# New order table, two loads swapped, copies split by PSUM bank, last tile in halves: one transformer block on one core

## The chip, the cores and the metric

The kernel runs on one core of one Trainium2 chip. The metric is the device time of one execution in microseconds (us). A core has five engines that run their own instruction streams: PE (TensorE, the matrix unit; its weight loads are counted apart as PEld), DVE (VectorE), ACT (ScalarE), POOL (GpSimd) and SP (SyncE, which only issues DMAs here). They wait for one another through semaphores. Each instruction stream is executed in order, so a waiting instruction holds up all that stands behind it on its engine.

## The reference

x has 2048 rows of 448 columns (bf16). One block is an attention with a learned feature map, and then a gated MLP that mixes over the rows; both are modulated by six vectors from a conditioning row c.

```python
mod = (silu(c) @ w_mod).reshape(1, 6, 1, 448)   # sa, ca, ga, sb, cb, gb
h = layernorm(x) * (1 + ca) + sa
x = x + ga * A(h)
h = layernorm(x) * (1 + cb) + sb
x = x + gb * B(h)

def A(h):        # 16 heads of 28
    q, k, v = split(h @ wqkv)
    phi(t) = concat(softmax(t @ w_phi), softmax(-(t @ w_phi)))   # per head
    kv, z = einsum(phi(k), v), sum over rows of phi(k)
    return (phi(q) @ kv) / (phi(q) @ z + 1e-6) @ wo

def B(h):
    z = gelu(h @ w_in)                     # 1792 columns
    z1, z2 = z[:896], layernorm(z[896:])
    return (z1 * (w_sp @ z2 + b_sp)) @ w_out
```

## The kernel before

The rows are cut into 16 tiles of 128 (number i below). The work runs in four stages.

1. Setup. The first loads go out on two DMA rings: ACT's (line 608: the last 64 rows of Wk, 56 KB; 610: x tiles 0 and 1, 224 KB; 611: part of w_mod) and SP's (607 c, 609 the other 384 rows of Wk, 613 w_phi, then w_mod, x and the weights of v and q through `load_rows`, which loads a 64-row piece and a 384-row piece). PE runs warm-up matmuls (`keep_busy`) and then `fold_T`: 16 transposes of Wk into two PSUM banks (`tps[0]` for groups g = 0 and 1, `tps[1]` for g = 2 and 3) and four copies out (line 742). Meanwhile DVE takes the statistics of x tiles 0 and 1, POOL makes the reciprocal deviations (`l1_rstd`, lines 680 to 684) and a product BD of w_phi with a mask (line 788), DVE applies the normalisation (line 690), and PE transposes the tiles (`turn_mm`; `turn_out` copies them into hT). `fold_pf` multiplies Wk by w_phi; `fold_W` scales the result into Wk. `columns` makes the modulation columns; `sapad`, `fold_sa` and the copy at 816 bring the shift into the last row of Wk's factor.
2. Keys and values, 3. attention output and 4. z. These are not written as loops but as a list of words, `ORDER`, which a loop at line 1191 plays: each word calls one step for one tile. The engine streams take their instructions in the order of this list, so the list fixes the order on each of the five engines at once.
5. Gating and output: for each of four column blocks of w_sp seven groups g_ps of 16 matmuls (line 1213), and 16 output tiles o_ps (1220). Tile 15 is the last: eight matmuls of 448 columns, the left half copied by ACT (1265), the right half by DVE (1267), each with its own store.

The words of the list, by engine:

- PE: k, v (key and value matmuls of a tile), kv (adds phi(k) x v into the accumulator kvacc), tm (transposes of an x tile), fq (transposes of Wq), sq, pq, bv, cfb, gt, gr, wb, zb (small matmuls for weights and biases), qp and q (queries), num (phi(q) @ kv), wo (output projection), z2 and z1 (the two halves of h @ w_in)
- ACT: e (two exponentials of k), vc (copies v), wv.0, wv.1 and bvc (the scaled value weights), gs (squares of Wk or Wq, lines 955 and 956; they only serve a flag that checks a bound), fqc, sqc, pqc, cfc, gtc, wbc, zbc, grc, qpe, qe (exponentials of q), sx, ge and zg (gelu), zn (normalises z2)
- DVE: bn, ag (statistics of x), ld1 (normalises tile 2 or 3), to, wv.2, wv.3, rd, rc, mu (softmax of k), wg, ws (scales wo and w_in), kb1, kb2 (kvacc into KVbd), cr, dn, ri, w, t (divides num), xc (adds the residual), ls, la, zs, za (statistics)
- POOL: rp, rs (reciprocal deviations), la1, ap (normalises a tile into a padded buffer), ad (adds the two halves of t into one of three buffers opad), ca, cc (constants)
- SP: ld (loads; 3 is x tiles 12 to 15, 4 is 840 KB of w_mod, 7 and 9 are 392 KB of it, 5 and 6 w_in, 8 wo), lT, oT, h2T (transposes of a tile by DMA: into hT, from opad, from the second layernorm), wsp.0 (eight transposing loads of w_sp's first block; they must all be there before g_ps starts)

A tile of the attention output goes num, sx, cr, dn, ri, w, t, ad, oT, wo, xc; then ls, la, rs, ap, h2T, z2, ge, zs, za; zn of tile i uses the rs of i + 3 (`ZL = 3`), and h2T of tile i + 3 comes out of the same rs. PSUM has a pool of four single banks (tag B: k, v, q, z1, wo and the small ones) and one of two double banks (tag A: kvacc, qp, num, z2); PE waits when the slot that it is to write has not been read yet. num.i holds its double bank until t.i.

Of the kernel before, what the change touches and what calls it, by code (L numbers as in the profile page):

```python
# [1320 lines left out]
```

## Time and profile before

| | us |
|---|---|
| median of 4 runs | 263.78 (262.85 to 264.59) |
| the profiled execution: device time | 263.19 |
| the profiled execution: span from first to last instruction | 261.4 |
| PE busy | 250.5 |
| DVE busy | 163.7 |
| PE busy at full clock, 20 to 60 | 40.0 of 40 |
| start of g_ps | 137.1 |
| end of the last matmul, about | 255.6 |

The page gives the busy time of each engine and its share; the windows give the same for a stretch. "Idle before" is the time an engine stood still ahead of an instruction, with the one that released it. The chain of waits is followed back from the last instruction: each row is a piece of time in which the end was held by that instruction. Ends of matmuls are modelled by the profiler, so two matmul rows may overlap by a tenth or two. The granted PE clock is 0.999 of full speed over the span.

### The profile page before, as it was taken

The numbers are of one execution on the slowest core, as the hardware profiler recorded it, in microseconds if no ns is written. First come the engines' busy times: TensorE is split into PE (matmuls) and PEld (weight loads), VectorE is DVE, ScalarE is ACT, GpSimd is POOL, SyncE is SP. The second block draws the span as 40 slices with busy tenths as digits, with TensorE's granted clock in tenths as the row PEclk, the third lists the DMA queues.
The fourth block names the chain that finished last, engine by engine and source line by source line (L and its number), as shares of the span: only waits on it lengthen the run. The fifth ranks groups of instructions, "written<-read, shape, count | busy, mean of one in ns | idle before, by whom it ended". The sixth has DMA issues, their size and how long they took to land.

```text
span 261.4 us, 4432 instructions
## 1 busy us (share of the span) xinstructions
PE 250.5 (96%) x1590; PEld 129.4 (50%) x1590; DVE 163.7 (63%) x364; ACT 107.9 (41%) x208; POOL 90.3 (35%) x201
## 2 busy tenths in 40 slices
PE   6889999999998999999999999999999999999991
PEld 3655666675554555544444444444444444444440
DVE  2889989999999989978062464432542534342540
ACT  2599777979775478887985000000000000000000
POOL 4787871004888778756340083000000000000000
PEclk9999999999999999999999999999999999999999
DMA  7975899506556334144499999950000010001002
GB/s 179 292 210 96 162 182 137 197 3 63 116 118 89 63 61 63 32 90 82 85 208 187 226 168 183 184 119 29 18 0 18 20 35 0 0 24 32 19 20 63
DMA packets 69057, 25.29 MB, mean 97 GB/s; under 512 B 59105, under 2 KB 68898, under 8 KB 69026
## 3 DMA queue, kind: packets, MB, share of 16 engines
q1 hardware_dynamic: 68066, 24.12, 46.2%
q10 hardware_dynamic: 960, 0.80, 1.1%
q8 instruction: 14, 0.23, 0.4%
q14 instruction: 17, 0.14, 0.2%
HBM read 8.92 MB, written 1.84 MB: 41 GB/s over the span
## 4 chain that ended last, share of the span: by engine, by line
PE 83%; DVE 6%; DMA 3%; ACT 3%; issue 2%; POOL 1%; ACTq 0%
PE g_ps L1213 37%; PE z_ps L832 17%; PE o_ps L1220 8%; PE v_ps L832 4%; PE k_ps L832 4%; PE x_ps L1105 3%; PE kvacc L866 3%; PE q_ps L832 2%; DVE t L1074 2%; DMA f_x<-in_A_x_dram 2%; DMA oT<-f_opad 2%; PE num L1045 2%; PE b_ps L778 1%; ACT f_Wsq L955 1%; ACT f_E L839 0%
## 5 line engine op out<-in xcount | busy, mean ns | idle before, releaser
L1213 PE MATMUL g_ps<-f_wsp,f_z2n 128*128 128x512 bf16 x336 | 74.3, 379 | 0.0
L1213 PEld LDWEIGHTS <-f_z2n 128*128 128x128 bf16 x448 | 43.7, 98 | 52.0
L1215 DVE TENSOR_TENSOR gb<-g_ps,f_bsp 128x512 f32<-128x512 f32 x28 | 19.4, 691 | 67.1 <-PE g_ps L1213 67.1
L1265 ACT CAST ot<-o_ps 128x224 bf16<-128x224 f32 x1 | 0.3, 346 | 114.6 <-PE o_ps L1220 114.6
L832 PE MATMUL z_ps<-f_win,h2T 128*128 128x448 bf16 (+1 forms) x128 | 26.9, 352 | 0.5 <-DMA h2T<-f_xpad 0.3
L1128 DVE BATCH_NORM_STATS2 z2st<-z2g 128x6 f32<-128x448 bf16 x32 | 19.2, 613 | 11.5 <-ACT z2g L1167 11.4
L832 PE MATMUL z_ps<-h2T,f_win 128*128 128x512 bf16 x112 | 26.2, 379 | 0.0
L1213 PE MATMUL g_ps<-f_hT,f_z2n 128*128 128x512 bf16 x112 | 25.0, 379 | 0.0
L1080 POOL TENSOR_TENSOR f_opad<-t 128x448 bf16<-128x448 bf16 x16 | 16.8, 1057 | 23.5 <-DVE t L1074 22.9
L1220 PE MATMUL o_ps<-f_wout,f_z1T 128*128 128x448 bf16 x112 | 23.5, 352 | 0.0
L1216 DVE TENSOR_TENSOR f_z1T<-gb,f_z1T 128x512 bf16<-128x512 f32 x28 | 21.1, 752 | 1.0
L1178 ACT ACTIVATE f_z1T<-z_ps,f_b 128x512 bf16<-128x512 f32 x28 | 18.2, 683 | 3.7 <-PE z_ps L832 3.7
L850 DVE TENSOR_REDUCE ksum<-f_E 128x32 f32<-128x896 bf16 x16 | 16.8, 1073 | 1.7 <-ACT f_E L839 1.5
L1171 ACT ACTIVATE f_z2n<-z2g,nm,rs 128x896 bf16<-128x896 bf16 x16 | 17.8, 1128 | 0.3 <-POOL nm L1142 0.3
L832 PEld LDWEIGHTS <-h2T 128*128 128x128 bf16 (+1 forms) x128 | 12.0, 97 | 11.8 <-DMA h2T<-f_xpad 0.8
L1167 ACT ACTIVATE z2g<-z_ps 128x896 bf16<-128x896 f32 x16 | 14.6, 919 | 6.6 <-PE z_ps L832 5.3
L832 PEld LDWEIGHTS <-f_win 128*128 128x128 bf16 x112 | 10.9, 97 | 12.8
L1074 DVE TENSOR_TENSOR t<-num,w 128x896 bf16<-128x896 f32 x16 | 17.0, 1084 | 0.1
L839 ACT ACTIVATE f_E<-k_ps 128x448 bf16<-128x448 f32 x32 | 16.1, 561 | 1.8 <-issue 1.1
L1220 PEld LDWEIGHTS <-f_z1T 128*128 128x128 bf16 x112 | 11.0, 98 | 10.9
L832 PEld LDWEIGHTS <-f_hT 128*128 128x128 bf16 (+1 forms) x128 | 11.5, 97 | 8.7 <-issue 0.5
L832 PE MATMUL v_ps<-f_Wv,f_hT 128*128 128x448 bf16 x64 | 14.6, 352 | 0.4 <-ACT junk L968 0.4
(148 smaller groups left out, 339.6 us busy)
## 6 DMA issues: line engine op xcount, KB each, us to landing
out_dram<-ot SPq DMA_DIRECT2D x15, 112.0 KB, 1.7
f_x<-in_A_x_dram SPq DMA_DIRECT2D x3, 448.0 KB, 7.0
f_win<-in_B_w_in_dram SPq DMA_DIRECT2D x2, 672.0 KB, 5.1
f_wm<-in_w_mod_dram SPq DMA_DIRECT2D x1, 840.0 KB, 6.9
f_wout<-in_B_w_out_dram SPq DMA_DIRECT2D x1, 784.0 KB, 6.0
f_bsp<-in_B_b_sp_dram SPq DMA_DIRECT2D x1, 512.0 KB, 5.0
f_wm<-in_w_mod_dram ACTq DMA_DIRECT2D x1, 448.0 KB, 6.1
f_wm<-in_w_mod_dram SPq DMA_DIRECT2D x1, 392.0 KB, 7.0
```

Source lines behind the costliest of these rows:

```text
L832: nc.tensor.matmul(out, lhsT=lhs(kc, last[kc]), rhs=rhs(kc, last[kc]), start=(kc == 0), stop=(kc == KC - 1))
L839: nc.scalar.activation(out=Ering[i % NR][:, s, :], in_=ps["k", i][:, 0:D], func=ACT.Exp, scale=1.0 - 2.0 * s)
L850: nc.vector.tensor_reduce(out=cs["s", i][:], in_=Ering[i % NR][:].rearrange("p s (c f h) -> p (s c) h f", c=4, h=HP), axis=AX.X, op=ALU.add)
L1074: nc.vector.tensor_tensor(out=ts[i][:, 0:2 * D].rearrange("p (s h d) -> p s h d", s=2, h=H), in0=nv(i)[:, :, :, 0:DH], in1=cs.pop(("w", i) ...
L1080: nc.gpsimd.tensor_tensor(out=opad[i % NO][:, 0:D], in0=t[:, 0:D], in1=t[:, D:2 * D], op=ALU.add)
L1128: nc.vector.bn_stats(out=cs["z", i][:, hf, :], in_=z2gs[i][:, hf * D:(hf + 1) * D])
L1171: nc.scalar.activation(out=z2n[:, i, :], in_=z2gs.pop(i)[:], func=ACT.Identity, scale=rstd[:, 1:2], bias=nmr[:, 1:2])
L1178: nc.scalar.activation(out=z1T[:, fc, st * 512:(st + 1) * 512], in_=ps.pop(("z1", st, fc)), func=ACT.Gelu_apprx_tanh, bias=b1[:, fc:fc + 1])
L1213: nc.tensor.matmul(g[:], lhsT=z2n[:, s_, fc * P:(fc + 1) * P], rhs=wsp_tiles[tcn][:, s_, :], start=(s_ == 0), stop=(s_ == NT - 1))
L1215: nc.vector.tensor_tensor(out=gb[:], in0=g[:], in1=bsp[:, tsl], op=ALU.add)
L1216: nc.vector.tensor_tensor(out=z1T[:, fc, tsl], in0=gb[:], in1=z1T[:, fc, tsl], op=ALU.mult)
L1220: nc.tensor.matmul(o_ps, lhsT=z1T[:, fc, t * P:(t + 1) * P], rhs=wout_s[:, fc, :], start=(first and fc == 0), stop=(fc == FC - 1))
```

## The change

On ACT's ring, x tiles 0 and 1 are loaded ahead of the 64-row piece of Wk. `load_rows` loads its big piece ahead of the small one. In `fold_T`, ACT copies both groups of the first bank and DVE both of the second, instead of one of each. POOL makes tile 0's and 1's reciprocal deviations before BD. The transposes of tile 1 stand ahead of `fold_pf` instead of behind `columns`, its copy out goes from DVE to ACT and stands behind `fold_sa`, and a filler matmul takes the old place. The statistics of tile 3 (bn.3, ag.3) leave the list and are taken with tile 2's. The last output tile is computed as two groups of 224 columns in two banks, and each half is copied and stored behind its own group. All other words of the list are the same and stand in another order. Of the list, the rows that matter most are shown.

```diff
@@ the table ORDER @@
-cc gs.0 k.0 bv bn.3 wv.2 ag.3 wv.1 bn.4 rp.1 gr.0 bn.5 bvc k.1 ld.7 wv.0 ag.4 wv.3 ag.5 ld.3 bn.7 grc.0 sq rp.2 e.0.0 bn.6 v.0 e.1.0 ld1.3 sqc ag.7
-e.1.1 ld1.2 tm.3 ag.6 bn.10 e.0.1 fq.0 la1.5 vc.0 to.3 fq.1 ag.10 rd.0 la1.4 fqc.2 lT.5 tm.2 k.3 fqc.0 rp.3 fqc.1 to.2 gt.0 rc.0 lT.4 fqc.3 bn.8 e.3.0
-k.2 mu.0 e.3.1 la1.7 rd.1 v.3 e.2.0 la1.6 lT.7 gtc.0 v.2 bn.9 e.2.1 ag.8 rc.1 k.4 vc.3 ag.9 lT.6 mu.1 rp.4 vc.2 pq.2 rd.2 v.1 e.4.1 ld.4 pqc.2 kv.0
-bn.12 vc.1 v.4 la1.8 bn.11 e.4.0 rc.2 pq.1 lT.8 pq.3 ag.12 vc.4 ag.11 k.5 rd.3 rp.5 pqc.1 k.6 pqc.3 mu.2 e.5.0 v.5 rc.3 rd.4 e.5.1 la1.9 pq.0 kv.1
-la1.11 bn.13 v.7 vc.5 mu.3 la1.10 lT.11 pqc.0 kv.2 ag.13 bn.15 k.7 rp.6 e.6.0 rd.5 e.6.1 lT.10 kv.3 v.6 rd.6 vc.7 la1.12 lT.9 qp.0 vc.6 rc.5 la1.13
...
-vc.14 zb mu.15 vc.15 wg.2 gs.1 wg.0 kv.14 wg.1 wg.3 kv.15 wb.3 kb1 wb.2 wbc.3 kb2 gr.1 wbc.2 ws.1 num.0 zbc num.1 ws.3 sx.0 q.5 sx.1 cr.0 cr.1 dn.0
-q.4 dn.1 ri.0 ri.1 qe.5.1 w.0 w.1 t.0 grc.1 q.6 qe.5.0 t.1 qe.4.1 q.12 ad.0 qe.6.0 num.3 qe.6.1 ws.2 ad.1 oT.0 num.2 qe.4.0 ws.0 q.9 sx.3 sx.2 qe.12.1
-cr.3 wsp.0.2 cr.2 q.7 dn.3 dn.2 qe.9.1 ri.3 ri.2 w.3 w.2 qe.9.0 q.8 t.3 qe.7.0 wsp.0.5 wo.0 qe.7.1 t.2 ad.3 qe.8.0 num.4 oT.1 xc.0 ad.2 num.5 sx.4
-q.10 cr.4 ls.0 sx.5 qe.12.0 oT.2 dn.4 cr.5 q.14 la.0 dn.5 ri.4 qe.10.1 rs.0 ri.5 w.4 w.5 qe.8.1 t.4 q.11 oT.3 wo.1 t.5 ad.4 qe.11.1 num.6 qe.11.0 xc.1
-ap.0 num.7 oT.4 sx.6 qe.10.0 q.13 cr.6 ls.1 ad.5 sx.7 qe.14.0 dn.6 q.15 cr.7 h2T.0 la.1 qe.14.1 dn.7 ri.6 rs.1 ri.7 w.6 qe.13.1 w.7 wo.2 t.6 qe.13.0
-wsp.0.3 wo.3 qe.15.0 ap.1 t.7 qe.15.1 num.8 ad.6 h2T.1 xc.2 z2.0 sx.8 tb cr.8 ad.7 dn.8 xc.3 oT.6 ri.8 ls.2 wo.4 ge.0 w.8 oT.5 la.2 t.8 gt.1 rs.2
-num.9 ls.3 oT.7 z2.1 zs.0.0 ap.2 sx.9 cr.9 la.3 dn.9 ad.8 zs.0.1 h2T.2 wo.5 ri.9 za.0 ge.1 w.9 xc.4 rs.3 wo.6 oT.8 t.9 num.10 zs.1.0 z2.2 ap.3 sx.10
-zn.0 cr.10 ls.4 ad.9 h2T.3 dn.10 zs.1.1 gtc.1 wo.7 ri.10 ge.2 la.4 w.10 oT.9 za.1 t.10 wo.8 rs.4 num.11 xc.5 z2.3 zs.2.0 sx.11 ap.4 zn.1 xc.6 ad.10
-xc.8 h2T.4 z1.0.2 ge.3 zs.2.1 ls.5 z1.0.1 oT.10 za.2 la.5 cr.11 xc.7 z1.0.3 rs.5 zs.3.0 z1.0.6 dn.11 ls.6 zg.0.3 ri.11 ap.5 z2.4 zs.3.1 zg.0.6 w.11
...
-ge.11 wsp.0.0 la.13 z1.2.5 rs.13 zs.11.0 z2.12 zg.2.5 zs.11.1 xc.14 ap.13 wo.15 ls.14 ge.12 h2T.13 za.11 la.14 z1.2.1 rs.14 xc.15 zn.9 zs.12.0 z1.2.0
-ls.15 zg.1.3 z1.2.6 ap.14 zs.12.1 zg.2.1 la.15 za.12 z1.2.2 h2T.14 rs.15 zg.2.6 zn.10 z1.2.4 z2.13 ap.15 zn.11 h2T.15 zn.12 z1.2.3 wsp.0.1 zg.2.0
-z2.14 zg.2.2 zg.2.3 wsp.0.4 zg.2.4 z1.3.4 ge.13 z1.3.5 wsp.0.7 ge.14 z1.3.6 zs.14.0 z2.15 zg.3.6 zs.14.1 zg.3.4 za.14 zs.13.0 rs.17 z1.3.1 ge.15
-zs.13.1 z1.3.3 za.13 zg.3.1 rs.16 zs.15.0 z1.3.2 zs.15.1 zg.3.3 zn.14 z1.3.0 za.15 rs.18 zg.3.2 zn.13 zn.15 zg.3.5 zg.3.0
+ca wv.3 rp.1 k.1 bv wv.0 wv.2 wv.1 bn.4 k.0 bvc bn.5 e.1.1 cc ag.4 ld.4 ld1.2 e.1.0 sq ag.5 bn.7 e.0.0 v.0 ld1.3 sqc ld.7 e.0.1 ag.7 bn.6 tm.2 tm.3
+vc.0 v.1 rp.2 to.2 gs.0 rd.0 k.2 to.3 v.2 rc.0 la1.5 bn.8 vc.1 v.3 bn.10 la1.4 vc.2 ag.6 e.2.0 fq.1 mu.0 rp.3 lT.4 e.2.1 fq.0 bn.9 vc.3 kv.0 ag.8 rd.1
+fqc.0 k.3 lT.5 fqc.2 la1.6 cfb bn.11 e.3.1 la1.7 rd.2 lT.6 e.3.0 gt.0 cfc fqc.3 rd.3 k.4 gtc.0 ld.3 gr.0 fqc.1 lT.7 ag.9 rc.2 e.4.1 rp.4 v.4 rc.1 rc.3
+grc.0 mu.1 k.5 vc.4 ag.10 mu.2 e.4.0 pq.1 la1.8 v.5 ag.11 e.5.0 rd.4 e.5.1 la1.9 pq.3 lT.8 kv.1 pqc.1 pq.2 rp.5 mu.3 kv.2 pqc.3 bn.13 k.6 wsp.0.4
+pqc.2 bn.12 vc.5 kv.3 ag.13 rd.5 la1.10 pq.0 e.6.0 v.6 lT.9 pqc.0 la1.11 rc.4 k.7 ag.12 rc.5 vc.6 rp.6 lT.11 mu.4 k.8 e.7.0 bn.15 e.6.1 v.7 lT.10
...
+rc.15 kv.13 mu.15 v.15 wg.1 wg.2 kv.14 wg.0 vc.15 wb.3 qpe.1.0 kv.15 wb.2 qpe.1.1 kb2 kb1 zb wbc.3 wg.3 gr.1 ws.2 num.0 num.1 ws.1 sx.0 q.7 zbc sx.1
+cr.0 wbc.2 cr.1 dn.0 q.5 dn.1 ri.0 ri.1 qe.7.1 w.0 w.1 t.0 qe.7.0 q.4 grc.1 t.1 qe.5.1 ad.0 num.3 qe.4.0 q.6 sx.3 ws.0 qe.4.1 ad.1 oT.0 num.2 cr.3
+ws.3 q.13 sx.2 qe.6.0 oT.1 cr.2 dn.3 q.12 dn.2 qe.5.0 ri.3 ri.2 w.3 qe.6.1 w.2 t.3 q.8 qe.12.1 t.2 wo.0 ad.3 qe.8.1 num.4 qe.12.0 xc.0 ad.2 num.5 sx.4
+q.10 cr.4 sx.5 ls.0 qe.8.0 oT.2 gt.1 dn.4 cr.5 ri.4 qe.10.0 dn.5 w.4 ri.5 q.9 la.0 qe.10.1 w.5 t.4 oT.3 rs.0 qe.13.1 wo.1 qe.9.0 t.5 num.6 gtc.1 ad.4
+xc.1 sx.6 num.7 ap.0 cr.6 q.14 ls.1 sx.7 qe.9.1 ad.5 dn.6 h2T.0 cr.7 la.1 q.15 dn.7 qe.13.0 ri.6 ri.7 w.6 qe.14.1 w.7 rs.1 t.6 wo.2 oT.4 qe.15.0
+qe.14.0 t.7 num.8 ap.1 qe.15.1 oT.5 wo.3 sx.8 xc.2 ad.6 tb z2.0 cr.8 xc.3 h2T.1 ad.7 dn.8 ls.2 ri.8 wo.4 oT.6 la.2 w.8 ge.0 ls.3 rs.2 wo.5 t.8 oT.7
+num.9 ap.2 zs.0.0 z2.1 sx.9 la.3 ad.8 h2T.2 cr.9 zs.0.1 dn.9 za.0 ri.9 wo.6 rs.3 w.9 oT.8 ge.1 xc.4 wo.7 t.9 num.10 ap.3 xc.5 z2.2 sx.10 zs.1.0 ad.9
+h2T.3 cr.10 ls.4 dn.10 wo.8 zs.1.1 oT.9 ge.2 ri.10 za.1 w.10 la.4 t.10 zn.0 rs.4 num.11 z1.0.0 ls.5 sx.11 zs.2.0 z2.3 ap.4 zg.0.0 cr.11 xc.6 ad.10
+h2T.4 dn.11 zs.2.1 z1.0.2 ri.11 ge.3 la.5 za.2 w.11 xc.8 rs.5 z1.0.3 zg.0.2 t.11 zn.1 num.12 z1.0.5 zs.3.0 ap.5 ls.6 sx.12 zg.0.3 z2.4 ad.11 zs.3.1
...
+ls.15 rs.13 wo.14 ge.11 z1.2.5 xc.14 zn.8 zs.11.0 ap.13 z2.12 ls.14 zg.2.5 h2T.13 zs.11.1 la.14 z1.2.2 za.11 ge.12 rs.14 z1.2.3 zg.2.2 zs.12.0 zn.10
+z1.2.4 la.15 zs.12.1 ap.14 z1.2.0 za.12 zg.1.3 h2T.14 rs.15 zg.2.3 z2.13 zg.2.0 zg.2.4 ap.15 z1.2.1 ge.13 h2T.15 z1.2.6 zg.2.1 zs.13.0 wsp.0.1 zn.11
+z2.14 wsp.0.5 z1.3.6 ge.14 z1.3.3 wsp.0.2 zg.3.6 zs.14.0 zn.12 z2.15 zs.14.1 wsp.0.0 za.14 zs.13.1 zg.3.3 rs.17 z1.3.1 za.13 ge.15 z1.3.5 rs.16 zg.3.1
+zs.15.0 z1.3.0 zs.15.1 zg.3.5 z1.3.4 za.15 zg.3.0 rs.18 zn.14 z1.3.2 zn.13 zn.15 zg.2.6 zg.3.2 zg.3.4
```

```diff
@@ -599,15 +599,15 @@
     wmod_v = w_mod.rearrange("(k p) n -> p k n", p=DC)
 
     def load_rows(eng, dst, src):
+        eng.dma_start(out=dst[:, 0:3, :], in_=src[0:3 * P, :].rearrange("(k p) n -> p k n", p=P))
         eng.dma_start(out=dst[0:64, 3, :], in_=src[3 * P:D, :])
-        eng.dma_start(out=dst[:, 0:3, :], in_=src[0:3 * P, :].rearrange("(k p) n -> p k n", p=P))
 
 
     nc.vector.memset(wk_raw[64:P, 3, :], 0.0)
     nc.sync.dma_start(out=c_row[:], in_=c)
-    nc.scalar.dma_start(out=wk_raw[0:64, 3, 0:D], in_=A_wqkv[3 * P:D, D:2 * D])
     nc.sync.dma_start(out=wk_raw[:, 0:3, 0:D], in_=A_wqkv[0:3 * P, D:2 * D].rearrange("(k p) n -> p k n", p=P))
     nc.scalar.dma_start(out=x_sb[:, 0:2, :], in_=xv[:, 0:2, :])
+    nc.scalar.dma_start(out=wk_raw[0:64, 3, 0:D], in_=A_wqkv[3 * P:D, D:2 * D])
     nc.scalar.dma_start(out=wm1[:, :, D:960], in_=wmod_v[:, :, D:960])
     with nc.allow_non_contiguous_dma(reason="small w_phi blocks"):
         nc.sync.dma_start(out=phi[:], in_=A_w_phi.rearrange("(g l) d f -> (l d) g f", l=4))
@@ -739,7 +739,7 @@
             for m in range(4):
                 nc.tensor.transpose(tps[g // 2][:, g % 2, m * P:(m + 1) * P], wraw[:, m, g * CB:g * CB + P], ident[:])
         for g in range(4):
-            (nc.vector.tensor_copy if g % 2 else nc.scalar.copy)(out=wT[:, g, 0:D], in_=tps[g // 2][0:CB, g % 2, 0:D])
+            (nc.vector.tensor_copy if g // 2 else nc.scalar.copy)(out=wT[:, g, 0:D], in_=tps[g // 2][0:CB, g % 2, 0:D])
 
     def fold_sa(wraw, sa_ps):
         for g in range(4):
@@ -785,10 +785,10 @@
     nc.vector.tensor_scalar(out=e[:], in0=e[:], scalar1=1.0, scalar2=None, op0=ALU.add)
     nc.vector.reciprocal(out=e[:], in_=e[:])
     nc.vector.tensor_tensor(out=scol[:], in0=e[:], in1=ctv, op=ALU.mult)
+    l1_rstd(0)
     nc.gpsimd.tensor_tensor(out=BD[:].rearrange("p g (f h) -> p g f h", h=HP),
                             in0=phi[:].unsqueeze(3).to_broadcast([CB, 4, DH, HP]),
                             in1=bmask[:].unsqueeze(1).unsqueeze(1).to_broadcast([CB, 4, DH, HP]), op=ALU.mult)
-    l1_rstd(0)
     more_constants()
     fold_T(wk_raw, wTk)
     l1_apply(0, nc.vector)
@@ -800,7 +800,7 @@
     nc.vector.memset(ca1[64:65, 3:4], 1.0)
     turn_mm(0)
     turn_out(0, hT[:, :, 0:P], True)
-    keep_busy(1, 256)
+    turn_mm(1)
     pf01 = bank2("pf01")
     for m in range(3):
         fold_pf(wTk, m)
@@ -810,15 +810,16 @@
     cf_s = bank("cf")
     columns(cf_s, wms, 128)
     nc.scalar.copy(out=sapad[:, :, 64], in_=cf_s[:, 0:4])
-    turn_mm(1)
+    keep_busy(1, 256)
     sa_ps = bank("sa_ps")
     fold_sa(wk_raw, sa_ps)
+    turn_out(1, hT[:, :, P:2 * P], True)
     nc.scalar.copy(out=wTk[:, :, D], in_=sa_ps[0:CB, 0:4])
     fold_pf(wTk, 3)
-    turn_out(1, hT[:, :, P:2 * P], False)
+    for i in (2, 3):
+        l1_bn(i)
+        l1_ag(i)
     fold_W(Wk, 3, True)
-    l1_bn(2)
-    l1_ag(2)
 
 
     Eq = eqp.tile([P, 4, 2, S], BF, name="f_Eq")
@@ -1251,7 +1252,7 @@
                 o_mm(o_ps[:, t % 2, 0:D], t, 0, FC)
                 o_fin(o_ps[:, t % 2, 0:D], t)
     tc.mark_branch_hint_location("general", hint="LikelyTaken")
-    last = [bank2("o_ps")[:, 0, 0:D] if n < 2 else bank("o_ps")[:, 0:D] for n in range(4)]
+    last = [bank2("o_ps")[:, 0, 0:D] if n < 2 else bank("o_ps")[:, 0:D if n == 2 else D // 2] for n in range(5)]
     for n in range(2):
         o_mm(last[n], 12 + n, 0, 6)
     for n in range(2):
@@ -1259,13 +1260,15 @@
         o_fin(last[n], 12 + n)
     o_mm(last[2], 14, 0, 7)
     o_fin(last[2], 14)
-    nc.tensor.matmul(last[3], lhsT=ident[:], rhs=x_sb[:, 15, :], start=True, stop=False)
-    o_mm(last[3], 15, 0, 7, first=False)
     ot = wk.tile([P, D], BF, tag="ot", bufs=4)
-    nc.scalar.copy(out=ot[:, 0:D // 2], in_=last[3][:, 0:D // 2])
-    nc.scalar.dma_start(out=outv[15][:, 0:D // 2], in_=ot[:, 0:D // 2])
-    nc.vector.tensor_copy(out=ot[:, D // 2:D], in_=last[3][:, D // 2:D])
-    nc.sync.dma_start(out=outv[15][:, D // 2:D], in_=ot[:, D // 2:D])
+    for n, (eng, copy) in enumerate(((nc.scalar, nc.scalar.copy), (nc.sync, nc.vector.tensor_copy))):
+        cols = slice(n * D // 2, (n + 1) * D // 2)
+        o_ps = last[3 + n]
+        nc.tensor.matmul(o_ps, lhsT=ident[:], rhs=x_sb[:, 15, cols], start=True, stop=False)
+        for fc in range(FC):
+            nc.tensor.matmul(o_ps, lhsT=z1T[:, fc, 15 * P:16 * P], rhs=wout_s[:, fc, cols], start=False, stop=(fc == FC - 1))
+        copy(out=ot[:, cols], in_=o_ps)
+        eng.dma_start(out=outv[15][:, cols], in_=ot[:, cols])
     wk.release()
     zp.release()
     wspB.release()
```

## The prediction

> **What bounds the kernel now.** I read the busy shares first, then the busy time by stretches, then the chain of waits, then the timeline of the first 20 us and of the end. TensorE (PE) carries the program:
>
> ```profile
> PE 250.5 (96%) x1590; PEld 129.4 (50%) x1590; DVE 163.7 (63%) x364; ACT 107.9 (41%) x208; POOL 90.3 (35%) x201
> ```
>
> So all that can be won is the time in which PE idles or does filler. By stretches (columns: window, its length, busy us of PE, PEld, DVE, ACT, POOL with counts, PE clock, DMA share, GB/s):
>
> ```profile
> 0.00:10.00 10.00, 7.67 (x65) 4.91 (x66) 4.62 (x18) 3.10 (x6) 6.06 (x40) 1.00 0.87 210
> 10.00:20.00 10.00, 8.66 (x124) 5.74 (x122) 8.81 (x25) 8.70 (x21) 7.89 (x28) 1.00 0.88 238
> 50.00:60.00 10.00, 10.00 (x131) 6.86 (x130) 9.45 (x25) 8.07 (x20) 0.08 (x1) 1.00 0.01 2
> 60.00:70.00 10.00, 9.58 (x75) 5.38 (x74) 10.00 (x27) 7.94 (x22) 6.32 (x8) 1.00 0.73 104
> 70.00:80.00 10.00, 9.88 (x72) 5.55 (x70) 9.90 (x33) 7.25 (x20) 8.00 (x14) 1.00 0.55 109
> 80.00:90.00 10.00, 9.13 (x58) 4.69 (x57) 10.00 (x26) 5.39 (x10) 8.16 (x18) 1.00 0.51 81
> 250.00:262.00 12.00, 5.58 (x30) 2.67 (x28) 3.55 (x6) 0.35 (x1) 0.00 (x0) 0.95 0.16 45
> ```
>
> PE is idle in three places: the start, the attention-output stage (60 to 90, where DVE has no free time), and the tail. The chain of waits (start, length, what) gives the links:
>
> ```profile
> 1.31 4.13 DMA f_x<-in_A_x_dram
> ...
> 12.81 1.31 ACT f_Wsq L955
> 14.12 0.47 ACT f_Wsq L956
> 14.58 0.56 ACT f_Wv L878
> ...
> 18.09 1.05 PE tps L887 x16
> ...
> 80.75 4.08 DMA oT<-f_opad
> 84.88 0.93 PE x_ps L1105 x4
> ...
> 121.46 15.84 PE z_ps L832 x76
> ```
>
> From 12.8 to 18.1 ACT is the chain, and 1.78 us of it is the squaring of Wk (step gs.0), which only a flag needs; V's weights (L878) wait behind it. At 84.88 PE waits for a transpose. The end:
>
> ```profile
> 255.66 0.35 ACT ot L1265
> 256.03 0.39 DVE ot L1267
> ```
>
> DVE's half is copied after ACT's, though both wait for the same matmul.
>
> **What the Trainium skill says.** "PSUM — Partial Sum Buffer" (PSUM bank collisions raise a hardware error): two engines on one bank must be kept apart by a semaphore, reads against reads included. The trace agrees: L1267 starts 0.02 us after L1265 ends. "SBUF — State Buffer" (SBUF: two separate sides): DVE's two-port modes and GpSimd hold one port pair exclusively. The trace agrees: the w_in scalings (L938) took 1.27 us for two with POOL quiet, 2.30 for two beside POOL's adds. "DMA: Bandwidth & Descriptors" (Anatomy of one DMA): about 2 us of a DMA are fixed, whatever its size. That section fits another issuing path; here 56 KB landed after 2.3 us, so I let order shift landings by tenths only. "TensorE: Matmul & The Clock Gate" (Back-to-back issue gap): N/2.4+2.5 ns; for 224 columns an estimate of 96 ns. Rows on both sides agree (448 columns 190 ns, 116 columns 52).
>
> **The start, part by part.** x tiles 0 and 1 go ahead of the 56 KB key piece on ACT's ring. Their issue moves from 1.31 to 0.73, and 56 KB leave the road in front, so they land at about 5.0 instead of 5.44. The key piece lands last, about 5.4; PE reads it as its fourth transpose, at 5.8, and the warm matmuls hold PE until 5.46 anyway: cost 0 (up to 0.5 if it slips). The statistics move 0.45 earlier (rstd on POOL at about 6.7, with the BD product, 0.93, now behind it, ending at 9.3), but the fold copies stop most of that. Split by bank, DVE's two copies (0.39 each) start when the second bank is transposed, 7.4, and end at 8.2 against 8.37. Then the two normalisations (0.99) end at 9.2 against 9.57. In the new code PE takes transpose 1 before the pf folds, so pf starts at 9.6 (now 9.42), BD just covered. From there ACT repeats its old row: W2, sapad, with turn_out(1) (0.58) under the 0.55 of sa; Wk's last piece ends at 12.93 (now 12.81). The edits ahead of the table are worth +0.1 by themselves, bounds +0.5 and -0.4; the lag below contains it.
>
> **The table.** I add durations of PE steps in table order (from the chain's rows: k, v, bv, wb, gt, wo 0.76; kv, num 0.42; q 0.87; qp 1.74; z2 1.52; z1 0.87; cfb 0.78; zb 0.68; sq 0.40; gr 0.38; tm, pq 0.2; fq 0.5). Both tables sum to 121.1. "Lag" is trace time minus this sum. Before: 14.1 after tm.3 (18.1) and still at kv.15 (54.6); 14.7 after num.5, which waited for t.2; 14.9 at z2.1, 15.3 at z2.2, 16.2 after wo.8, and 16.2 to the end (137.30). The first step could start at 12.07, so 4.1 us is lost.
>
> After, the start: ACT has wv.0, wv.1, bvc (0.56+0.56+0.45) straight after 12.93, so Wv is whole at 14.5 (now 16.4), gs.0 comes after vc.0. PE finishes k.1 at 13.2: lag 12.45. bv, k.0, sq bring v.0 to 15.1, after Wv. DVE, counted from 12.6 with bn/ag 3 moved ahead: ld1.2 at 14.4 (POOL's rp.1 12.65 to 14.3, constants now behind it), ld1.3 15.4, to.2 16.4, mu.0 20.0; PE reaches kv.0 at 20.4. ACT ends e.2.1 at 20.4, just when k.3 wants its bank. PE's lag stays 12.5. The later kv steps stand 1.0 to 2.5 us behind their mu. SP now has the 840 KB reload first, then lT.4, lT.5, lT.6, and only then x tiles 12 to 15 (ld.3), at about 23.1; bn.13 wants them at 27.8. Nearest row: f_x from SP, median 7.0 in the crowded start; wm's 840 KB at 23.6 took 6.9; I take 5, and 2.4 us of kv slack covers a later one. The two wsp pieces added before 35 us stand behind lT.8 and lT.10; hT tiles have over 1 us there.
>
> The middle: kv.15 ends at 41.4+12.5 = 53.9 (now 54.6). DVE then does kb2, kb1, wg.3, ws.2, ws.1 (0.2+1.0+0.3+1.4) and reaches cr.0 at 56.9 (now 57.35). ws.0 and ws.3 beside POOL's adds cost 0.95 over their row. DVE's own lag is then 15.5 (now 15.85 at t.2, 16.1 at t.10). What counts is how far the table keeps PE's consumers behind DVE: before, 1.3 us in the sums (t.2 to num.5, t.9 to num.10, t.10 to z2.3), so PE's lag could not fall under 16.1-1.3 = 14.8; after, 2.0 to 2.5 (t.6 to num.8, t.10 to z2.3, t.12 to num.13), so 13.0 to 13.5. And oT.8: before, ad.8 waited 0.66 for oT.5 (behind oT.6 in SP's queue), then landed after 4.1. After, oT.4 to oT.7 are in order and three wsp pieces have left the stretch; t.8 ends at 76.9, ad.8 at 78.3, oT.8 is issued at 78.5 and lands at 81.0 to 82.6, wo.8 wants it at 81.9: 0.3.
>
> Then the loop z2.i, gelu, statistics, rs, ap, h2T, z2.(i+3): 8.45 us in the trace (z2.12's end 120.5 to h2T.15's landing 128.95), and the table leaves 8.2 between z2.12 and z1.3.6: 0.3. Other h2T stand 0.3 to 0.7 us free; I take another 0.3. End lag 13.5+0.3+0.3+0.3, about 14.4 (range 13.0 to 15.6): 1.8 us before today's 16.2. The last wsp piece now follows h2T.15 as fourth, not third: issued about 129.7, landing 3.7 to 7.4 later, and PE starts g_ps at about 135.5. Cost 0, at most 1.6.
>
> **The tail.** Eight 448-column matmuls become sixteen of 224: 16 x 0.096 against 8 x 0.19, +0.02. ACT's half is copied under PE's second half; DVE's copy starts at once after the last matmul, like ACT's now: 0.37 earlier. Its 56 KB store landed after 3.1, ACT's is out of the way. -0.35 (bounds 0 and -0.5).
>
> **Sum.** Start and table together -1.8, tail -0.35: -2.15; the 118 us of g_ps and o_ps between them are untouched and full. On the profiled execution's own 263.19 (span 261.4 and 1.8 around it) that is 261.0; this execution lies 0.59 under the median 263.78 of the runs, so against the median it is 261.6, my forecast.
>
> **Rivals.**
> 1. DVE binds the middle as now, and only its own gain (0.45) and the tail (0.35) come through: 263.0. For it: DVE is at 10.00 and 10.00 in 60 to 70 and 80 to 90. Against: PE's consumers stand further back in the new sums. 0.17.
> 2. No stall after the start: lag 12.5 to the end, -3.7-0.35: 259.7. Against: DVE's lag of 15.5 with 2.0 of distance. 0.10.
> 3. Slower. The loop through h2T is run five times from z2.0 to z2.15, with about 0.3 us free each. If a transpose lands later than 2.8 us in it, each turn pays: at 4.0, the longest seen for h2T, 5 x 1.2 = 6.0 against 2.15 won: 267.6; it decides from a mean landing of 3.5, where the sum passes +1.3. For it: SP issues in order, and 4.1 was seen at oT.8. Against: the median is 2.5 and the wsp pieces left this stretch. 0.12.
>
> **How the numbers follow.** A measurement can tell about 0.5% (1.3 us) from no change. My case (0.61; its own spread 260.2 to 262.5) and rival 2 (0.10) are faster, rival 1 is within, rival 3 mostly slower: faster 0.70, same 0.18, slower 0.12. The range takes in rival 1 and leaves out half of rival 2 and nearly all of rival 3: 259.9 to 263.4.
>
> **What will show it.** Right: PE's first v at about 15 (now 16.7); continuous PE from about 13; kv's end near 53.9; the z phase ending near 135.5; no wait of L1105 on oT over 0.5; the DVE half copied within 0.1 of the last matmul. Wrong: a wait of DVE for x around 28; PE waits on t or h2T of over 2 us in total between 57 and 130; a wait for wsp ahead of g_ps; tps waiting for the key piece.

## The result, and the profile after

The changed kernel takes 262.33 us (median; the kernel before, on the same chip, 263.27). The ratio is 0.9962, 95% interval 0.9948 to 0.9975: about 1.0 us faster. Timed once more beside the experiments it gave 262.11 and a ratio of 0.9956 (0.9934 to 0.9978). In some executions PE runs part of the start at half clock and the time is 2 to 6 us longer; the ratios leave out those over 1.5% above the kernel's fastest, and the profile below is of an execution without it.

The lines below are of that second measurement, whose profiled execution took 261.88 (span 260.0). The busy shares first:

```profile
PE 248.9 (96%) x1578; PEld 130.0 (50%) x1598; DVE 161.2 (62%) x363; ACT 108.5 (42%) x209; POOL 92.4 (36%) x201
```

Then the stretches (window, its length, busy us of PE, PEld, DVE, ACT and POOL with counts, PE clock, DMA share, GB/s):

```profile
10.00:20.00 10.00, 9.35 (x107) 5.73 (x104) 9.68 (x26) 9.03 (x20) 7.14 (x20) 1.00 0.95 252
60.00:70.00 10.00, 9.47 (x72) 5.25 (x71) 9.84 (x27) 8.06 (x22) 6.02 (x8) 1.00 0.35 54
70.00:80.00 10.00, 9.85 (x68) 5.40 (x67) 9.97 (x33) 6.66 (x18) 8.54 (x15) 1.00 0.46 80
80.00:90.00 10.00, 8.56 (x58) 4.55 (x57) 9.99 (x27) 5.46 (x11) 8.13 (x17) 1.00 0.47 68
```

From 10 to 20 PE is busy 9.35 us instead of 8.66: the hole of the start has shrunk. From 80 to 90 it is 8.56 instead of 9.13: there the time is given back. The chain of waits says at what (start, length, what):

```profile
21.87 3.58 DMA f_hT<-f_xpad
25.50 0.93 PE k_ps L833 x4
...
72.24 3.33 DMA oT<-f_opad
75.70 1.03 POOL f_opad L1081
...
80.19 4.25 DMA oT<-f_opad
84.49 0.93 PE x_ps L1106 x4
...
123.66 4.13 DMA h2T<-f_xpad
127.84 9.29 PE z_ps L833 x44
```

Four transposing DMAs stand in the chain, three of them (oT, oT, h2T) for the attention output and z, with landings of 3.3 to 4.3 us; the median of such a DMA in this trace is 2.4 to 2.5. The table below gives starts and PE's lag (trace time minus the sum of PE's steps in table order, as in the prediction), in us. The last column is of an experiment told below.

| step | before | forecast | after | PE program shifted (e9) |
|---|---|---|---|---|
| v.0 starts | 16.72 | 15.1 | 15.14 | 14.88 |
| kv.15, lag | 14.1 | 12.5 | 12.9 | 12.9 |
| wo.0, lag | 14.0 | | 13.6 | 12.9 |
| z2.2, lag | 15.3 | 13.0 to 13.5 | 14.1 | 13.7 |
| wo.8, lag | 16.0 | plus 0.3 | 15.7 | 13.7 |
| g_ps starts | 137.14 | 135.5 | 136.97 | 135.50 |

So the start came as forecast, and nearly all of it was lost again: g_ps starts 0.2 earlier than before. What was won stands behind it. The chain now ends with

```profile
254.75 0.69 PE o_ps L1269 x7
255.43 0.02 issue
255.46 0.39 DVE ot L1270
```

DVE's copy starts 0.02 us after the last matmul, and its store is issued at 255.88, 0.44 after it, where it was 0.86 before (256.45 after 255.59). The store also lands sooner (before, then after; the last figure is us from issue to landing):

```profile
out_dram<-ot SPq DMA_DIRECT2D x1, 56.0 KB, 3.1
out_dram<-ot SPq DMA_DIRECT2D x1, 56.0 KB, 2.1
```

From the end of the last matmul to the end of the span it is 5.8 us before and 4.6 after. All kept traces agree: 5.3 to 5.8 in the four with the old tail (before, e2, e4, e5), 4.4 to 4.9 in the ten with the new one, about 0.85 less on average. By the traces, then, the tail carries nearly all of the 1.0 us.

### The profile page after: what moved, and what is told of

Read it like the earlier page. It is cut to its first block, busy times and chain, and to the rows that moved or that the text cites. A ratio compares the mean times of both kernels' runs of the same rounds, so it can differ in the third digit from the quotient of the medians.

```text
span 263.2 us, 4453 instructions
## 1 busy us (share of the span) xinstructions
PE 252.6 (96%) x1598; PEld 131.1 (50%) x1598; DVE 163.3 (62%) x363; ACT 108.5 (41%) x209; POOL 91.4 (35%) x201
## 4 chain that ended last, share of the span: by engine, by line
PE 85%; DMA 5%; DVE 3%; issue 2%; POOL 2%; ACT 1%; ACTq 0%; POOLq 0%
PE g_ps L1214 37%; PE z_ps L833 14%; PE o_ps L1221 8%; PE k_ps L833 5%; PE v_ps L833 5%; PE q_ps L833 3%; DMA oT<-f_opad 3%; PE x_ps L1106 3%; PE kvacc L867 3%; DMA h2T<-f_xpad 2%; PE num L1046 1%; PE warm_ps L673 1%; DVE t L1075 1%; PE b_ps L778 1%; DVE f_xpad L690 1%
## 5 line engine op out<-in xcount | busy, mean ns | idle before, releaser
L1216 DVE TENSOR_TENSOR gb<-g_ps,f_bsp 128x512 f32<-128x512 f32 x28 | 19.4, 692 | 69.2 <-PE g_ps L1214 63.9
L833 PE MATMUL z_ps<-h2T,f_win 128*128 128x512 bf16 x112 | 26.9, 379 | 0.0
L1221 PE MATMUL o_ps<-f_wout,f_z1T 128*128 128x448 bf16 x105 | 22.0, 352 | 0.0
L1217 DVE TENSOR_TENSOR f_z1T<-gb,f_z1T 128x512 bf16<-128x512 f32 x28 | 19.7, 702 | 1.2
L840 ACT ACTIVATE f_E<-k_ps 128x448 bf16<-128x448 f32 x32 | 15.4, 548 | 1.9 <-ACT f_vaug L847 0.9
L833 PE MATMUL k_ps<-f_Wk,f_hT 128*128 128x448 bf16 x64 | 15.9, 379 | 0.0
L1106 PE MATMUL x_ps<-f_wo,oT 128*128 128x448 bf16 x64 | 14.4, 352 | 1.4 <-DMA oT<-f_opad 1.4
```

The costliest lines, as they stand in the source:

```text
L833: nc.tensor.matmul(out, lhsT=lhs(kc, last[kc]), rhs=rhs(kc, last[kc]), start=(kc == 0), stop=(kc == KC - 1))
L1106: nc.tensor.matmul(ps["x", i][:, 0:D], lhsT=oT[:, cc, :], rhs=wo_s[:, cc, :], start=(i in RES_DVE and cc == 0), stop=(cc == KC - 1))
L1216: nc.vector.tensor_tensor(out=gb[:], in0=g[:], in1=bsp[:, tsl], op=ALU.add)
L1217: nc.vector.tensor_tensor(out=z1T[:, fc, tsl], in0=gb[:], in1=z1T[:, fc, tsl], op=ALU.mult)
L1221: nc.tensor.matmul(o_ps, lhsT=z1T[:, fc, t * P:(t + 1) * P], rhs=wout_s[:, fc, :], start=(first and fc == 0), stop=(fc == FC - 1))
```

## The experiments

### Was it POOL's memset at the start?

In the first profile of the changed kernel (265.0 us, one of the executions with a disturbed start) the normalisation of x tiles 0 and 1 ran into POOL's step ca (it clears padded buffers; the memset of L651 is its longest), which the new table has as its first word. Timeline (start, length, engine, line; in brackets the wait):

```profile
8.38 2.53 DVE L690 TENSOR_SCALAR f_xpad<-f_x,rstd,nmr 128x448 bf16<-128x448 bf16 x2
9.18 1.60 POOL L651 MEMSET f_win<- 64x1792 bf16 x1
10.97 0.40 PE L729 MATMUL t_ps<-f_ident,f_xpad 128*128 128x128 bf16 x4 [1.26 <-DVE f_ca L799]
```

and by stretches PE then stood still and came back at half clock:

```profile
10.00:11.00 1.00, 0.03 (x1) 0.03 (x2) 0.98 (x2) 0.33 (x1) 0.78 (x1) 1.00 1.10 315
12.00:15.00 3.00, 2.65 (x41) 1.84 (x39) 2.93 (x9) 2.00 (x6) 0.27 (x1) 0.50 1.01 254
```

Three runs ask whether that is the general loss: the changed kernel again (e0), with ca put back (e1), and the kernel before with ca moved forward (e2).

> The changed kernel once more, as the measure for the next three. Ratio to before 0.996 (262.3 against 263.3). In its start the pair of normalisations of x tiles 0 and 1 takes about 2.5 us for two, beside POOL's 1.60 us memset; the first pf matmul is at about 11.2, and PE's clock either stays at 1.00 or falls to 0.5 for some us after 12.

> The changed kernel with step ca (POOL's memsets of the padded constants, 1.60 us the longest) put back behind la1.15. Theory, the memset holds the port that DVE needs for the normalisations: the pair takes 1.0 instead of 2.53 us, pf starts at 9.5 to 9.9 instead of 11.2, PE has no gap of over 1 us at 10, its clock stays at 1.00, and no execution is at 264 or above; the time is 260.8 (1.5 under the changed kernel). Rival, DVE or the transposes bind the middle and absorb an earlier start: pf starts as early, but the time is 262.0 to 262.3.

> The kernel before with step ca issued on POOL ahead of BD, nothing else. Theory (port): the two normalisations go from 0.99 to about 2.5 us for two, pf starts 1.0 to 1.5 later than 9.42, and the time is 264.3 to 264.8, with a lower PE clock in some executions. Rival (the start has slack behind it): within 0.3 of before.

```diff
# e1, in ORDER
-ca wv.3 rp.1 k.1 ...
+wv.3 rp.1 k.1 ...
-... kv.5 la1.15 k.10 ...
+... kv.5 la1.15 ca k.10 ...
# e2, in the setup of the kernel before (and ca out of ORDER)
     l1_rstd(0)
+    constants_a()
     more_constants()
```

e0: 0.9956. In its trace the pair is done before the memset begins:

```profile
8.02 0.81 DVE L690 TENSOR_SCALAR f_xpad<-f_x,rstd,nmr 128x448 bf16<-128x448 bf16 x2
9.25 1.59 POOL L651 MEMSET f_win<- 64x1792 bf16 x1
```

so my expectation of 2.5 us for the pair did not come: it took that where DVE came 0.36 us later, in the first profile. e1: 0.9974 (0.9941 to 1.0007), no better than e0, though the pair takes 1.44 instead of 2.53 and pf starts at 9.85, as expected; and three of its 11 executions lie above 264, where the theory expected none. e2: 1.0035 (1.0019 to 1.0051), 0.9 us slower. But not as the theory said: the pair does stretch (2.06 us), and yet pf starts at 9.44 as before. The chain goes through POOL's own queue, from nmr (the normalisation's shift, made on POOL at 8.34) into the memset, over three small memsets that e2 puts behind it, to ACT's copy sapad, which starts at 11.39 instead of 10.82:

```profile
8.89 1.68 POOL f_win L651
11.39 0.18 ACT f_sapad L813
```

In the changed kernel these small memsets stand ahead of ca, so e2's 0.9 us is not the price of the collision with DVE alone; that price is not shown. As e0 has no collision and the same loss, and e1 without the early memset is no better, the memset is not what swallowed the gain.

### The parts alone

> The kernel before with the last output tile alone computed in column halves, each in its own bank. Theory: DVE's half is copied within 0.1 of the last matmul and its store issued 0.3 to 0.4 earlier, 0.35 won: ratio 0.9987. Rival (the end is the landing of a store with a fixed cost, and sixteen matmuls cost more than eight): within 0.1 of before.

> The kernel before with the new order table alone (step ca kept behind la1.15, bn.3 and ag.3 ahead of the table's first step); loads, fold copies and tail are the old ones. Theory, the table gives back in the attention-output stage what it wins at the start (DVE full from 60 to 90, then oT.8 and h2T.15 each landing after over 4 us): g_ps starts within 0.3 of the kernel before, and the time is 262.7 to 263.0, ratio 0.998 to 0.999. Rival, my prediction's sum (table -1.8): 261.2, ratio 0.993.

> The kernel before with the edits ahead of the table alone (x tiles ahead of the key piece, copies split by bank, rstd ahead of BD, second turn moved, bn and ag of tile 3 moved forward); old table, old tail. Prediction: +0.1, bounds +0.5 and -0.4, so 263.1 and a ratio of 0.999 to 1.002. Rival, the earlier x carries through to the end (statistics done 1.9 earlier, pf at 9.2 or before): ratio 0.997 or less.

Each is the kernel before with the hunks of that part from the diff above:

```diff
# e3: the kernel before, with
-    last = [bank2("o_ps")[:, 0, 0:D] if n < 2 else bank("o_ps")[:, 0:D] for n in range(4)]
+    last = [bank2("o_ps")[:, 0, 0:D] if n < 2 else bank("o_ps")[:, 0:D if n == 2 else D // 2] for n in range(5)]
...
# e4: the kernel before, with the new ORDER (ca back behind la1.15), which begins
+bn.3 ag.3 wv.3 rp.1 k.1 bv wv.0 ...
# e5: the changed kernel, with the old tail and the old ORDER without its bn.3 and ag.3
```

| part | ratio | 95% interval | us |
|---|---|---|---|
| tail alone (e3) | 0.9984 | 0.9967 to 1.0001 | -0.4 |
| table alone (e4) | 1.0006 | 0.9989 to 1.0022 | +0.2 |
| setup alone (e5) | 1.0016 | 0.9995 to 1.0036 | +0.4 |
| all, with ca early (e0) | 0.9956 | 0.9934 to 0.9978 | -1.2 |

The tail's ratio agrees with the forecast (-0.35), and its interval also takes in the 0.85 us that the traces show. The setup edits are inside their bounds (+0.5, -0.4). The table, forecast at -1.8 together with the setup, brings nothing by itself, although its trace shows the early start (v.0 at 15.00) without any setup edit. It has the same wait as the changed kernel: oT at 80.08 lands after 4.25, x_ps waits 1.4; g_ps starts at 136.84. The three add up to 1.3 us more than the whole (0.9 with the tail as in the traces), somewhat more than their intervals explain; that stays open.

### What makes those transposes late: one packet

Queue q8 carries 14 packets of 16 KB in the whole execution (page: "q8 instruction: 14, 0.23, 0.4%"). Between 55 and 130 us there are four: in the kernel before they begin in the microseconds 64, 81, 102 and 125; in the changed one at 62.0, 81.0, 101.8 and 125.3 (in steps of a quarter). Each time a transpose in flight lands late: 3.9, 4.1, 3.4, 4.0 us before, 3.2 to 3.7, 4.3, 3.0, 4.1 after. (The 3.33 at 72.24 in the chain meets a packet of another queue, q14, of 8 KB at 73.7; q14's packets make fewer transposes late.) This is the DMA view of the changed kernel from 81 to 83 us, in 40 slices (first row: mean busy tenths of 16 engines):

```profile
DMA  0009000147999999999999999000000000000010
GB/s 0 0 0 328 0 0 0 26 82 169 215 200 200 205 195 215 189 210 205 195 87 42 21 0 0 0 0 0 0 0 0 0 0 0 0 0 5 5 10 10
q8 instruction: 1, 0.02, 5.2%
oT<-f_opad SPq DMA_TRANSPOSE x1, 4.3
```

The packet is the single 9 at 81.15. The transpose oT.8 then moves its data from 81.35 to 82.1 on all engines, but a remainder of 5 to 10 GB/s follows only from 82.8 on. The packet's time, 5.2% of 16 engines in 2 us, is 1.7 us of one engine, which fits a transpose that waits for one engine's share: 81.15 and 1.7 give 82.8, where the remainder begins.

All fourteen kept traces together say the same. They give the landing of 402 oT and h2T transposes. A q8 packet begins within 2.1 us after the issue of 50; 48 of these land after 3.0 us or more, and the median is 3.9. Only a q14 packet begins so for 60; 28 are late, median 2.7. Neither does for 292; 5 are late, median 2.4, and with four of those five a q8 packet that began earlier was still under way.

That these packets fetch PE's instructions was a guess; the Trainium skill, "Runtime: NRT & Kernel Launch" (Instruction fetch mechanics), says that each engine's sequencer drives a DMA queue of its own and refills in blocks of 16 KiB, 256 instructions, at a cost that is mostly hidden. If so, more PE instructions ahead must move them; e6 tests it. A rival is that DVE, full from 60 to 90, holds PE; e7 tests it by leaving out DVE's scaling of w_in (its result is thus not the block's). e8 has both edits.

> The changed kernel with the 7 warm-up matmuls of 512 columns at the start as 56 of 64 columns: the same columns streamed, but 98 PE instructions more ahead of everything, so that each 16 KB packet of queue q8 (one every 20 us from 62 on, taken for PE's instruction fetch) falls 98 of 256 instructions, about 7 to 8 us, earlier in PE's program. Theory, the packet is what makes oT.8 land after 4.25 us: the packets move to about 73, 94 and 117, oT.8 and the late h2T land after 2.4 to 2.7, the wait of x_ps for oT falls from 1.4 to under 0.4, and the time is 260.5 to 261.3. Rival, oT.8 is slow for another reason (its place in SP's queue, the data): landing 4.2 and wait 1.4 as before, time 262.0 to 262.4.

> The changed kernel without the scaling of w_in by 1 + c (step ws, DVE, 3.8 us in four instructions at 57 to 66); the rest of the computation stays. Theory, DVE binds PE between 57 and 84: PE's z2.0 ends 0.8 to 1.4 earlier than 75.99, and behind the wait for oT.8 0.5 to 1.0 of it is left at the end: 261.2 to 261.6. Rival, the transposes alone bind: z2.0 earlier but the wait for oT.8 longer by the same amount, time 262.0 to 262.3.

> The changed kernel with both earlier edits at once: without the scaling of w_in by 1 + c on DVE (3.8 us of DVE at 57 to 66 left out), and with the 56 small warm-up matmuls that move queue q8's packets 5 to 10 us earlier. Apart they brought nothing (262.05) and 0.3 (261.77) against 262.1. Theory, two bounds in series that cover each other (DVE full from 57 to 90, and transposes that a q8 packet delays): with both gone the sum of PE's idle time from 57 to 100 falls by 1 or more, time 260.6 to 261.2. Rival, a third bound (POOL's chain through ad, rs and ap, or ACT's) holds PE: 261.6 to 262.1.

```diff
# e6
-    keep_busy(7)
+    for _ in range(56):
+        nc.tensor.matmul(wps[0:16, 0, 0:64], lhsT=ident[:, 0:16], rhs=..., start=True, stop=True)
# e7
     def ws_(kk):
-        nc.vector.tensor_scalar(out=win_s[0:KD[kk], kk, :], in0=win_s[0:KD[kk], kk, :], ...)
+        pass
# e8: both
```

e6: the packets move to 56, 76.3, 94 and 115.8, and the late landings go with them. oT.8, issued at 80.4, lands after 2.4 and has no wait; h2T.14, 4.1 in e0, lands after 2.4. But others are hit now (chain of e6):

```profile
74.44 3.98 DMA h2T<-f_xpad
78.47 1.69 PE z_ps L834 x8
```

PE waits 0.8 for this h2T and 0.5 in z further on (there for DVE), and an oT issued at 93.0 lands after 4.2. The ratio is 0.9979 (0.9959 to 0.9999): nothing won. So the packet is the cause of the late landing, and its removal from oT.8 alone does not pay, because it falls on h2T.1 instead.

e7: 261.77 us, between the two expectations; ratio 0.9951 (0.9937 to 0.9964), the same as e0 within the intervals, with 3.8 us less of DVE's work. DVE simply waits more from 55 to 70 (line waited for: us in total, times, longest):

```profile
DVE cr L1056 <- ACT Sx L1052: 1.2, 2, 1.1
DVE cr L1056 <- ACT f_b L936: 1.2, 1, 1.2
```

and PE gets no further:

```profile
64.67 0.92 PE L1106 MATMUL x_ps<-f_wo,oT 128*128 128x448 bf16 x4 [0.56 <-issue]
```

wo.0 starts at 64.67, in e0 at 64.62. The profile names no releaser, but oT.0, which wo.0 reads, is issued at 60.76 and lands after 3.82, at 64.58: it meets the packet at 62. DVE's work is therefore not what held PE there, although DVE was full.

e8: 0.9962 (0.9942 to 0.9982), which is not better than either. Its profiled execution waits 2.4 us for w_mod at the start, and the shifted packet (76.2), with one of q14 (75.9), again hits an oT (4.4; PE waits 1.2 for it) and an h2T (3.8). It does not separate the two theories.

### Moving the packet to where nobody waits

In the changed kernel oT.9, issued at 84.02, is wanted only at 93.5. A shift by 208 PE instructions, 48 short of a whole block, brings each packet nearly to where the one ahead of it was (in the trace 2.0 to 6.5 us behind that place): one comes beside oT.9.

> The changed kernel with 104 PE matmuls (208 PE instructions with their weight loads) more at the start, in the same streamed columns, so that q8's packets fall 208 instructions earlier, which is 48 later than the changed kernel's: at about 66, 84.5, 105 and 129, beside oT.9 (wanted 7 us after it lands) instead of oT.0 and oT.8. Theory: wo.0 starts at about 63.9 (now 64.62), oT.8 lands after 2.4 to 2.6 and its wait is under 0.3; what DVE doesn't take back is won: 261.0 to 261.7. Rival (DVE takes all of it, as in the first shift): 262.0 to 262.3.

> The changed kernel with step wo.8 moved behind num.11 and z1.0.0 in the table (0.42 and 0.87 of PE work that stood behind it now stand ahead of it). Theory: PE's wait for oT.8 falls from 1.4 to about 0.1 and the z phase ends 0.5 to 1.3 earlier: 260.9 to 261.6. Rival, num.11 or z1.0.0 isn't ready there (DVE's t.10, ACT's zn.0), or DVE takes it back: 262.0 to 262.3.

```diff
# e9: 104 more, smaller fillers for the same streamed columns
-    keep_busy(7)
+    keep_small(86, 41)
...
-    keep_busy(2)
+    keep_small(20, 51)
...
-    keep_busy(1, 256)
+    keep_small(8, 32)
# keep_small(n, cols): n matmuls, lhsT=ident[:, 0:16], cols columns
# e10, in ORDER
-... dn.10 wo.8 zs.1.1 ... num.11 z1.0.0 ls.5 ...
+... dn.10 zs.1.1 ... num.11 z1.0.0 wo.8 ls.5 ...
```

e9: 261.38 us, ratio 0.9922 (0.9901 to 0.9942): under the kernel before, and under the changed kernel's 0.9962 (0.9948 to 0.9975); e0's interval it just touches. The packets come in the half microseconds from 68.5, 85.0, 103.5 and 128.5. The same view as above, around oT.8 (79.8 to 82.4), has no packet and no remainder:

```profile
DMA  9999999942000000001599999998530000000000
oT<-f_opad SPq DMA_TRANSPOSE x1, 2.4
```

wo.0 starts at 63.90 (expected 63.9), and wo.8 and g_ps at:

```profile
82.57 0.92 PE L1110 MATMUL x_ps<-f_wo,oT 128*128 128x448 bf16 x4
135.50 2.75 PE L1218 MATMUL g_ps<-f_wsp,f_z2n 128*128 128x512 bf16 x11
```

with no wait for oT. oT.9 meets the packet and lands after 4.0, and nothing waits for it. The smaller fillers are not the reason: they start pf 0.7 earlier (8.78 against 9.50), but kv.15 ends at 54.45 against 54.53 in e0. DVE is as full as ever, and yet PE is ahead:

```profile
80.00:90.00 10.00, 9.60 (x65) 5.16 (x64) 9.99 (x26) 6.21 (x14) 8.24 (x17) 1.00 0.31 63
```

e10: 0.9964 (0.9944 to 0.9984), nothing won. Where wo.8 stood, num.11 now waits 1.0 for ACT's z2g, and z_ps 0.5 for an h2T: the rival's case, so this order does not cover the late landing. (In its profiled execution PE was busy only 2.5 of the 4 us from 82 to 86, and its clock was 0.50 from 86 to 88, so its size is not to be relied on.)

The last run takes back one setup edit in e9.

> The kernel of the 208-instruction shift with one edit of the change taken back: on ACT's ring the key piece stands ahead of x tiles 0 and 1 again. Theory: x tiles first make the c columns of w_mod (448 KB behind them on that ring) land late in part of the executions (5.9 to 8.5 us after issue, against 5.6 to 6.1 with the key piece first), PE then idles before cf and runs some us at half clock; with the key piece first w_mod lands after 5.6 to 6.2, at most 2 of 22 executions are over 263.5 (9 of 22 before this edit), and as x lands 1.3 later the undisturbed ones lose 0 to 0.5 against 260.99: median 261.0 to 261.5. Rival, the late executions come from something else: again a third or more of them near 265, median 261.4 or more.

```diff
# e11
-    nc.scalar.dma_start(out=x_sb[:, 0:2, :], in_=xv[:, 0:2, :])
     nc.scalar.dma_start(out=wk_raw[0:64, 3, 0:D], in_=A_wqkv[3 * P:D, D:2 * D])
+    nc.scalar.dma_start(out=x_sb[:, 0:2, :], in_=xv[:, 0:2, :])
```

261.95 us, ratio 0.9954 (0.9931 to 0.9976), against 0.9922 with x first: more lost than the 0 to 0.5 us expected. The intervals overlap, so that x first helps is likely and not settled. The trace is a second one with the packets moved (70.1, 86.7, 105.4), and it repeats e9 where they matter: oT.8 lands after 2.4, and from the end of kv.15 (56.01) to g_ps

```profile
137.08 3.19 PE L1218 MATMUL g_ps<-f_wsp,f_z2n 128*128 128x512 bf16 x14
```

PE takes 81.1 us, in e9 81.0, in e0 and e6 82.4. What e11 loses against e9 it loses at the start (pf at 10.19 instead of 8.78).

Two of its 14 executions were above 263.5 (highest 263.8), against 9 of 22 (highest 266.06) in e9, whose mean over all executions, 262.6, is therefore no better than e0's 262.2. The fewer late ones fit the theory; its mechanism does not: w_mod landed after 7.2 here too, and PE waited 1.2 for it, without a fall of the clock. What throws some executions into half clock stays open.

## Why the prediction was right, and where it was not

The forecast was 261.6, and 262.33 came: inside the range, on the right side. But against the kernel before it was to win 2.15 us and won 1.0, under half. Its good place owes 0.5 us to luck, the median of the first four runs, 263.78, which later runs put at 263.27, and more to two errors that partly cancelled: in the traces, start and table together, booked at -1.8, brought 0.2 at g_ps, and the tail, booked at -0.35, about 0.85. The call that it would be faster by over 0.5% (0.70) did not come.

- Start: right in the result. pf starts at 9.50 (forecast 9.6), v.0 at 15.14 (15.1), kv.0 at 20.6 (20.4), fold copies done at 8.1 (8.2). Two terms inside were off and cancelled out. x landed at 3.4, not 5.0 (2.7 us after issue instead of 4.1), and the key piece 3.9 us after issue instead of 2.3, so the transposes of Wk start at 5.46 as before. "Cost 0" for the key piece held.
- Missed: I looked only at what stands behind the memsets on POOL and not at the DVE instruction beside them. In the first profile, where they met, pf started at 11.20.
- kv.15: it ended at 54.4, against 53.9. k.4 was 0.2 late, and k.5 another 0.25 behind the hT transpose of 3.58.
- The middle: the step that failed is the one for oT.8, "oT.8 is issued at 78.5 and lands at 81.0 to 82.6, wo.8 wants it at 81.9: 0.3". It was issued at 80.19 and landed at 84.44; the wait was 1.4. I had taken the 4.1 us seen in the trace of before for an accident of the queue, ad.8 waiting behind oT.6, and let order cure it. It was a packet tied to PE's program. oT.0, with a landing of 3.7, I did not price at all. With the packets moved away (e9) the forecast lags nearly come out: 13.7 at z2.2 against 13.0 to 13.5, and g_ps at 135.50 against 135.5. The account of the middle was right in its order of waits, and its mis-sized term is the landing: 0.3 booked, some 1.5 at g_ps.
- Tail: -0.35 forecast; e3 measured -0.4 (-0.9 to 0.0). The earlier issue came as booked (0.42 against 0.37), but I kept the store's landing at 3.1, and in the ten traces with the new tail it took 2.1 to 2.4. So the traces show about 0.85. Why the store lands sooner is not shown.
- Last wsp piece: cost 0, as forecast; PE shows no wait for it.
- Rival 1 (DVE binds, -0.8) is nearest in size to the measured -1.0, but its reason falls with e7 and e9: DVE full and PE ahead. Rival 2 (no stall) did not come, and e9 stays 1.9 above its lag of 12.5. Rival 3 named the right kind of thing, transposes landing at 4, but in the loop of h2T; there three landed late in e0 (3.0, 3.4 and 4.1), and from wo.8 to g_ps the lag grew by 0.2 in all.

## What to carry to other kernels

When one DMA of a kind lands far above its median, look at what else moves in the same microsecond, the instruction queues included, before blaming the order; and ask whether that traffic follows the clock or the program. If it follows the program, instructions added or removed far ahead move it, for better (e9) or for nothing (e6). An engine that is full is not yet the bound: take work from it, and see whether anything behind it starts earlier. And when a gain comes, ask from the trace which stage it came in: here the stage that was to bring it gave 0.2 us.

## What the runs showed of the hardware

- One 16 KB packet of queue q8 lengthens a transposing DMA that it meets from 2.4 to as much as 4.3 us. It moved with PE's instruction count (98 more: from 81.0 to 76.3; 208 more: the one at 101.8 to 85.0), while in e6 and e9 q14's packets stayed within 1 us of 73, 88 and 91. That fits the skill's account of PE's instruction fetch; its "mostly hidden" does not tell of the DMA met on the way, for which PE waited 1.4 us in e0.
- PE's clock was 0.50 from 12 to 18 us in the first profile, after PE had waited 1.26 us up to 10.97, but stayed at 1.00 after 2.4 us of waiting in e8. The skill, "TensorE: Matmul & The Clock Gate" (What's actually happening), puts the fall after an idle window of about 3.4 us, and has results that vary from run to run. The first case fell after a shorter wait than that; what decides is not shown here.
- Two DVE normalisations took 2.53 us beside a 64x1792 memset on POOL (1.60 us; first profile) and 2.06 in e2, against 0.81 (e0) and 1.44 (e1) with that memset at another time.
- The last store, 56 KB, landed 2.5 to 3.1 us after its issue in the four traces with the old tail, where it was issued 0.42 after ACT's, and 2.1 to 2.4 in the ten with the new one, 0.77 after it.
